# Reordering the first loads of a two-layer transformer kernel: Wq in four pieces, Wv ahead of the transposing DMAs, softmax of group 0 one unit earlier

## The chip, the cores and the metric

The kernel runs on one core of one Trainium2 chip. The metric is the device time of one execution in microseconds (us); lower is better. "Before" is the kernel without the change, "after" the kernel with it.

Engine names are those of the profile: PE is TensorE (matmuls), PEld its weight loads, DVE is VectorE, ACT is ScalarE, POOL is GpSimd, SP is SyncE, which here only issues DMAs (SPq in the traces).

## The reference, cut to what matters

```python
def _A_ref(x, wqkv, wo):                 # attention, 32 heads of 32, window of 8 keys, dilation 2
    qkv = (x @ wqkv) ...
    logits = einsum(q, gathered k) * scale, masked for positions before 0
    o = softmax(logits) @ gathered v
    return o.reshape(B, S, D) @ wo

def _B_ref(x, w1, b1, w2, b2):           # feed-forward, F = 3584
    return gelu(x @ w1 + b1) @ w2 + b2

x = A_x                                  # 1 x 2048 x 1024, bf16
x = x + _A_ref(_layernorm(x), A_wqkv, A_wo)
x = x + _B_ref(_layernorm(x), B_w1, B_b1, B_w2, B_b2)
# ... and the same two lines once more, with the same weights
```

## The kernel before: the parts that matter

The 2048 rows are handled as four groups of 512 rows, that is of four tiles x0 to x3, x4 to x7 and so on, 128 rows each. A group needs Q, K and V (8 chunks of 128 columns each), then the windowed attention on DVE, then Wo. PE is kept in program order; for the other engines a scheduler picks an order when the kernel is built, except where program order is demanded: POOL is in program order from the start on (`pool.on = True`).

```python
x = [xpool.tile([P, D], BF16, name=f"x{t}") for t in range(S // P)]

def load_x(g):                                   # four tiles of 256 KB, on SP
    for tt in range(NTT):
        t = g * NTT + tt
        sp.dma_start(x[t][:], x_in[t * P:(t + 1) * P, :])

load_x(0)

def load_qkv(which):                             # 0 is Wq, 1 is Wk, 2 is Wv; two halves of 1 MB, on SP
    tiles = []
    for h in range(2):
        wt = wpool.tile([P, KD // 2, D], BF16, name="wt")          # 5 buffers
        sp.dma_start(wt[:], wqkv_v[:, h * (KD // 2):(h + 1) * (KD // 2), which * D:(which + 1) * D])
        tiles.append(wt)
    return tiles

wq_first = load_qkv(0)
# ... cut ...

def build_constants():
    pool.memset(zhalo[:], 0.0)                   # zeros for the halo of the first group
    # ... cut: other small constants on POOL ...

def load_bias():
    b1_rows = attp.tile([KF, P], BF16, name="abc")
    pool.dma_start(b1_rows[:], B_b1.rearrange("(j p) -> j p", p=P))        # issued by POOL
    pool.dma_start(b2bc[:], B_b2.unsqueeze(0).to_broadcast([P, D]))
    ps = psum.tile([P, KF], BF16, name="acc", bufs=6)
    pe(nc.tensor.transpose(ps[:], b1_rows[:], ident[:KF, :KF]))            # PE waits for b1 here
    act.copy(b1T[:], ps[:])
```

A layer norm of one tile goes DVE (statistics), POOL (two tiny instructions that make `rstd`), DVE (the norm `xn`, three buffers), and then, for every group but the first, a transposing DMA on SP that reads `xn` and writes `xnT`. So DVE may write the norm of a tile only when the transposing DMA of three tiles back has landed.

```python
def ln_stats(t, mv=None, rstd=None, between=None):
    # ... DVE: bn_stats twice, bn_aggr ...
    pool.tensor_tensor(out=rstd[:], in0=mv[:, 1:2], in1=eps_t[:], op=ALU.add)
    pool.tensor_tensor(out=rstd[:], in0=rstd[:], in1=mhalf[:], op=ALU.pow)
    return mv, rstd

def ln_norm(t, mv, rstd):
    xn = lnp.tile([P, D], BF16, name="xn", bufs=3)
    vec.tensor_scalar(out=xn[:], in0=x[t][:], scalar1=mv[:, 0:1], scalar2=rstd[:], op0=ALU.subtract, op1=ALU.mult)
    return xn

def ln_tile(t, tt, xnT, on_pe=False, ahead=False):
    # ... cut ...
    sp.dma_start_transpose(xnT[:, tt, :, :], xn[:].rearrange("s (k p) -> s k p", p=P))
```

The first group is transposed on PE instead, and its first Q chunks are computed from the first two tiles while the other two are still on their way:

```python
def gen_qkv(n, parts=1, defer=False, qk_pool=None, v_late=False):
    # ... cut ...
    wq = wq_first if n == 0 else load_qkv(0)
    wk = load_qkv(1)
    qT = qk_pool.tile([P, NCH, T], BF16, name="qT")
    first = {}
    for kh in range(2 if n == 0 else 0):               # two half passes over the first two tiles
        for c in range(6):
            first[c] = qkv_chunk(wq, c, xnT, first.get(c), kh * (KD // 2), (kh + 1) * (KD // 2), 0, 2)
            if kh == 1 and c in (0, 3):
                transpose_on_pe(*first_late.pop(0))    # the third and the fourth tile
    for c in range(NCH):                               # "the next pass": the other two tiles
        ps = qkv_chunk(wq, c, xnT, first[c], t0=2) if c in first else qkv_chunk(wq, c, xnT)
        act.copy(qT[:, c, :], ps[:])
        yield
    if not v_late:
        wv = load_qkv(2)
    kT = qk_pool.tile([P, NCH, HALO + T], BF16, name="kT")
    s["qT"], s["kT"] = qT, kT
    act.copy(kT[:, :, 0:HALO], (zhalo if g == 0 else khalo)[:])
    # ... cut: K (8 units), V (8 units), one yield per chunk ...
```

DVE multiplies Q with the shifted K (`new_prod`, 2.2 us each) and adds the products in pairs; `head_sum` is a group of PE matmuls that sums a product over each head. The first head sum stands behind the fourth V chunk in PE's program order, so PE stops there if DVE is not ready. A `stage` runs one generator unit by unit and hangs side work on units:

```python
pool.on = True
warm_up(16)
ln_first()
build_constants()
with tc.tile_pool(name="early", bufs=1) as early:
    load_x(1)
    stage(gen_qkv(0, 2), sides=at(0, load_x, 2) + at(0, ln_a, 1) + at(1, load_x, 3) + at(6, ln_a, 2, early)
          + at(14, load_bias) + at(19, head_sum, 0, False))
    q1 = gen_qkv(1, 2, defer=True, qk_pool=early)
    stage(q1, sides=at(6, attend, 0) + at(6, spread, 0) + at(6, hold) + each(new_prod, 1, 8, 1, 0, 4) + each(av, 0, 12, 1))
    # ... cut ...
```

`attend(0)` makes the softmax of group 0.

## Time and profile before

| what | value |
|---|---|
| time before, median of 3 runs | 1247.69 us (1247.63 to 1249.89) |
| span of the profiled execution | 1246.4 us |
| PE busy | 1236.3 us (99%) |
| PE waiting for the Wqkv loads | 5.4 us, three times |
| first projection matmul | 10.36 us |
| next pass begins | 17.04 us |
| first head sum on PE | 53.62 us |

Two lines of the page: PE's busy time from its first part, and the shares of the chain of waits that ended last.

```profile
PE 1236.3 (99%) x5871; PEld 633.3 (51%) x5871; DVE 836.2 (67%) x864; ACT 305.9 (25%) x477; POOL 95.2 (8%) x215
...
PE 98%; DMA 1%; SPq 0%; ACT 0%; issue 0%; DVE 0%
```

PE is what bounds the kernel, and there is little left but what keeps PE from working at full rate. PE's waits say what that is (engine, the tile waited with, line; what it waited for; us in total, times, longest).

```profile
PE acc L118 <- DMA wt<-in_A_wqkv_dram: 5.4, 3, 2.5
PE acc L118 <- DVE big L93: 1.1, 1, 1.1
PE acc L118 <- ACT xnT L93: 0.2, 1, 0.2
```

The 1.1 us for DVE's big tile are the warm-up's first operand. The 5.4 us are found in PE's timeline (start, us, engine, line, operation, shapes, count, and in brackets the idle time just before and what ended it).

```profile
10.36 3.37 PE L118 MATMUL acc<-xnT,wt 128*128 128x256 bf16 x28 [1.45 <-DMA wt<-in_A_wqkv_dram]
...
17.04 20.94 PE L118 MATMUL acc<-xnT,wt 128*128 128x256 bf16 x120 [0.22 <-ACT xnT L93]
...
41.44 1.09 PE L118 MATMUL acc<-xnT,wt 128*128 128x512 bf16 x4 [1.46 <-DMA wt<-in_A_wqkv_dram]
45.03 8.66 PE L118 MATMUL acc<-xnT,wt 128*128 128x512 bf16 x28 [2.51 <-DMA wt<-in_A_wqkv_dram]
53.62 0.61 PE L118 MATMUL L<-big,smat 128*32 128x512 bf16 x8
```

The waits are 1.45 us at Wq, 1.46 and 2.51 us at the two halves of Wv. Then 28 matmuls take 8.66 us, which is 0.31 us each. The table by stretches says why (stretch, its length, busy us and instructions of PE, PEld, DVE, ACT, POOL, the granted TensorE clock, DMA share, GB/s).

```profile
40.00:50.00 10.00, 6.05 (x16) 2.52 (x17) 9.83 (x6) 1.74 (x4) 0.00 (x0) 0.66 0.95 340
```

The granted clock was 0.66 there. In shorter stretches it was 1.00 for the four matmuls between the two waits (41.44 to 42.53 us), 0.62 during the second wait, 0.50 from 45.03 to 49.70 us, where weight loads start 0.43 us apart, and 0.96 from 49.70 to 53.60. So in this trace two waits of 4.0 us in all are followed by 4.7 us of matmuls at half the clock.

Why the halves of Wv are late is in SP's timeline: they are issued at 33.31 and 36.99 us, behind transposing DMAs (DMA_TRANSPOSE), for `load_qkv(2)` comes after all of Q in the program.

```profile
17.22 7.80 SPq L93 DMA_TRANSPOSE xnT<-xn  x3
...
33.31 0.85 SPq L93 DMA_DIRECT2D wt<-in_A_wqkv_dram  x1
34.25 2.65 SPq L93 DMA_TRANSPOSE xnT<-xn  x1
36.99 4.67 SPq L93 DMA_DIRECT2D wt<-in_A_wqkv_dram  x4
```

DVE's timeline: the norms of x7 and x8, at 25.48 us, wait for nothing; DVE waits once, 1.80 us at the norm of x10, for a transposing DMA to free a norm buffer, and the last two additions for the first head sum end at 47.64 us, 6 us before PE gets there.

```profile
25.48 0.99 DVE L93 TENSOR_SCALAR xn<-x,mv,rstd 128x1024 bf16<-128x1024 bf16 x2
...
30.70 0.63 DVE L93 TENSOR_SCALAR xn<-x,mv,rstd 128x1024 bf16<-128x1024 bf16 x1 [1.80 <-DMA xnT<-xn]
...
43.02 4.62 DVE L93 TENSOR_TENSOR big<-big 128x4096 bf16<-128x4096 bf16 x2
```

### The profile page before, as it was taken

Reading aid. Unit: us, or ns where it says so; the run is one execution under the profiler, and the core shown is the slowest. Engines: PE = TensorE matmul, PEld = TensorE weight load, DVE = VectorE, ACT = ScalarE, POOL = GpSimd, SP = SyncE. Lnnn points to the kernel's source line nnn. Section 1 sums busy time; section 2 is a strip of 40 time slices with the busy share of each in tenths; the row PEclk is TensorE's granted clock in tenths of the full one; section 3 lists DMA queues with packets and bytes.
Section 4 is the critical chain, followed back from the end, with each engine's and each line's share of the span. In section 5 each row is a group of like instructions: output and inputs, shape, how many; then the busy total and the mean of one; then the engine's idle time right before and its main releaser. Section 6 shows DMA issues by size and latency. Waiting matters only on the chain.

```text
span 1246.4 us, 14107 instructions
## 1 busy us (share of the span) xinstructions
PE 1236.3 (99%) x5871; PEld 633.3 (51%) x5871; DVE 836.2 (67%) x864; ACT 305.9 (25%) x477; POOL 95.2 (8%) x215
## 2 busy tenths in 40 slices
PE   9899999999999999999999999999999999999998
PEld 6566544446444564445644456444554444444444
DVE  7969889996995889528994379943598688012001
ACT  3233253013430135201352013510235101310310
POOL 4010112002001100101001010000000002000000
PEclk9899999999999999999999999999999999999999
DMA  9755554586746547656566555666654567546441
GB/s 301 215 191 188 142 190 155 166 206 189 199 147 202 169 137 208 184 165 159 169 185 199 165 164 173 161 198 193 199 155 146 181 202 193 166 155 195 147 138 53
DMA packets 215296, 219.83 MB, mean 176 GB/s; under 512 B 66034, under 2 KB 184960, under 8 KB 212160
## 3 DMA queue, kind: packets, MB, share of 16 engines
q1 hardware_dynamic: 212560, 208.16, 55.7%
q0 software_dynamic: 2672, 10.76, 2.8%
q8 instruction: 46, 0.75, 0.2%
q14 instruction: 18, 0.15, 0.0%
HBM read 197.40 MB, written 6.29 MB: 163 GB/s over the span
## 4 chain that ended last, share of the span: by engine, by line
PE 98%; DMA 1%; SPq 0%; ACT 0%; issue 0%; DVE 0%
PE acc L118 98%; DMA wt<-in_A_wqkv_dram 1%; PE L L118 0%; SPq L93 0%; ACT xnT L93 0%; PE L L206 0%; PE acc L206 0%; DVE x L93 0%
## 5 line engine op out<-in xcount | busy, mean ns | idle before, releaser
L118 PE MATMUL acc<-xnT,wt 128*128 128x512 bf16 (+1 forms) x3376 | 725.6, 377 | 5.6 <-DMA wt<-in_A_wqkv_dram 5.4
L118 PEld LDWEIGHTS <-wt 128*128 128x128 bf16 x3376 | 398.3, 119 | 329.0 <-issue 6.9
L118 PE MATMUL acc<-wt,hT 128*128 128x512 bf16 (+1 forms) x1820 | 388.1, 376 | 0.0
L118 PEld LDWEIGHTS <-hT 128*128 128x128 bf16 x1820 | 178.2, 98 | 208.9
L93 DVE TENSOR_TENSOR big<-big 128x2048 bf16<-128x2048 bf16 (+2 forms) x182 | 239.6, 1349 | 1.6
L93 ACT ACTIVATE hT<-acc,b1T 128x512 bf16<-128x512 f32 x224 | 151.6, 687 | 318.5 <-PE acc L118 318.0
L93 DVE TENSOR_TENSOR big<-abc,vT 128x4096 bf16<-128x4096 bf16 x64 | 143.9, 2283 | 48.5 <-DMA abc<-a_d 48.5
L93 DVE TENSOR_TENSOR big<-qT,kT 128x4096 bf16<-128x4096 bf16 x64 | 144.1, 2286 | 26.4 <-ACT kT L93 23.3
L93 DVE TENSOR_TENSOR tmp<-acc,b2bc 128x512 f32<-128x512 f32 x56 | 38.7, 691 | 178.4 <-PE acc L118 174.7
L93 ACT CAST qT<-acc 128x512 bf16<-128x512 f32 x64 | 37.2, 585 | 328.4 <-PE acc L118 328.4
L118 PE MATMUL acc<-wt,oT 128*128 128x512 bf16 x448 | 97.9, 379 | 0.0
L93 DVE BATCH_NORM_STATS2 stats<-x 128x6 f32<-128x512 bf16 x128 | 84.1, 677 | 4.4 <-DMA x<-in_A_x_dram 3.5
L118 PEld LDWEIGHTS <-oT 128*128 128x128 bf16 x448 | 43.8, 98 | 53.0 <-issue 0.2
L93 DVE TENSOR_TENSOR x<-acc,big 128x512 bf16<-128x512 f32 (+1 forms) x9 | 5.7, 632 | 90.0 <-PE acc L118 90.0
L93 ACT CAST vT<-acc 128x512 bf16<-128x512 f32 x64 | 37.5, 586 | 91.6 <-PE acc L118 91.6
L93 DVE TENSOR_SCALAR xn<-x,mv,rstd 128x1024 bf16<-128x1024 bf16 x60 | 32.7, 546 | 34.1 <-POOL rstd L93 31.3
L93 ACT CAST kT<-acc 128x512 bf16<-128x512 f32 x64 | 37.5, 585 | 72.1 <-PE acc L118 72.1
L93 POOL TENSOR_TENSOR rstd<-mv,eps_t 128x1 f32<-128x1 f32 x60 | 15.1, 251 | 501.4 <-DVE mv L93 501.4
L93 POOL DMA_DIRECT2D a_d<-a x32 | 19.5, 636 | 414.1 <-DVE a L93 414.1
L93 DVE TENSOR_TENSOR x<-acc,x 128x512 bf16<-128x512 f32 x64 | 43.0, 671 | 6.2 <-PE acc L118 5.9
L93 DVE TENSOR_TENSOR x<-tmp,x 128x512 bf16<-128x512 f32 x56 | 38.7, 691 | 1.7
L93 POOL TENSOR_TENSOR rstd<-rstd,mhalf 128x1 f32<-128x1 f32 x60 | 33.8, 563 | 4.7
(54 smaller groups left out, 213.0 us busy)
## 6 DMA issues: line engine op xcount, KB each, us to landing
wt<-in_B_w_dram SPq DMA_DIRECT2D x56, 1024.0 KB, 6.0
wt<-in_B_w_dram SPq DMA_DIRECT2D x64, 896.0 KB, 4.9
wt<-in_A_wqkv_dram SPq DMA_DIRECT2D x48, 1024.0 KB, 5.7
wt<-in_A_wo_dram SPq DMA_DIRECT2D x16, 1024.0 KB, 5.0
abc<-a_d POOLq DMA_DIRECT2D x32, 256.0 KB, 4.9
x<-in_A_x_dram SPq DMA_DIRECT2D x16, 256.0 KB, 6.8
out_dram<-x SPq DMA_DIRECT2D x31, 128.0 KB, 1.8
a_d<-a POOLq DMA_DIRECT2D x32, 64.0 KB, 3.4
```

Of the source, the lines that this page charges most:

```text
L93: inst = f(*args, **kwargs)
L118: return pe(nc.tensor.matmul(*args, **kwargs))
```

## The change

The intent: take PE's 5.4 us of waiting for weights away, and the low clock that follows. Wq's halves come in two pieces each, placed between the first x tiles, and the first pass goes by quarters to match. Wv of group 0 is issued together with Wk and the third group of x, ahead of the transposing DMAs. As PE would then run ahead, the softmax of group 0 is placed at unit 5 of the next group instead of 6.

```diff
-    def load_x(g):
-        for tt in range(NTT):
+    def load_x(g, t0=0, t1=NTT):
+        for tt in range(t0, t1):
...
-    load_x(0)
+    def load_qkv_half(which, h, pieces=1):
+        wt = wpool.tile([P, KD // 2, D], BF16, name="wt")
+        n = KD // 2 // pieces
+        for i in range(pieces):
+            k = h * (KD // 2) + i * n
+            sp.dma_start(wt[:, i * n:(i + 1) * n, :], wqkv_v[:, k:k + n, which * D:(which + 1) * D])
+        return wt
...
-    wq_first = load_qkv(0)
+    load_x(0, 0, 2)
+    wq_first = [load_qkv_half(0, 0, 2)]
+    load_x(0, 2, 4)
+    wq_first.append(load_qkv_half(0, 1, 2))
...
         norm(0)
-        stats[2] = ln_stats(2, between=lambda: norm(1))
+        norm(1)
+        stats[2] = ln_stats(2)
...
         wk = load_qkv(1)
+        if n == 0:
+            load_x(2)
+            wv = load_qkv(2)
...
-        for kh in range(2 if n == 0 else 0):
+        for kq in range(4 if n == 0 else 0):
             for c in range(6):
-                first[c] = qkv_chunk(wq, c, xnT, first.get(c), kh * (KD // 2), (kh + 1) * (KD // 2), 0, 2)
-                if kh == 1 and c in (0, 3):
+                first[c] = qkv_chunk(wq, c, xnT, first.get(c), kq * (KD // 4), (kq + 1) * (KD // 4), 0, 2)
+                if (kq, c) in ((2, 3), (3, 1)):
                     transpose_on_pe(*first_late.pop(0))
...
-        if not v_late:
+        if n > 0 and not v_late:
             wv = load_qkv(2)
...
-        stage(gen_qkv(0, 2), sides=at(0, load_x, 2) + at(0, ln_a, 1) + at(1, load_x, 3) + at(6, ln_a, 2, early)
+        stage(gen_qkv(0, 2), sides=at(0, ln_a, 1) + at(1, load_x, 3) + at(6, ln_a, 2, early)
...
-        stage(q1, sides=at(6, attend, 0) + at(6, spread, 0) + at(6, hold) + ...
+        stage(q1, sides=at(5, attend, 0) + at(5, spread, 0) + at(5, hold) + ...
```

More of the change, by code (lines that the diff above doesn't have):

```diff
@@ L120 @@
     x = [xpool.tile([P, D], BF16, name=f"x{t}") for t in range(S // P)]
-    def load_x(g):
-        for tt in range(NTT):
+    def load_x(g, t0=0, t1=NTT):
+        for tt in range(t0, t1):
             t = g * NTT + tt
             sp.dma_start(x[t][:], x_in[t * P:(t + 1) * P, :])
-    load_x(0)
-    def load_qkv(which):
-        tiles = []
-        for h in range(2):
-            wt = wpool.tile([P, KD // 2, D], BF16, name="wt")
-            sp.dma_start(wt[:], wqkv_v[:, h * (KD // 2):(h + 1) * (KD // 2), which * D:(which + 1) * D])
-            tiles.append(wt)
-        return tiles
-    wq_first = load_qkv(0)
+    def load_qkv_half(which, h, pieces=1):
[5 more added lines that the diff above has]
+        return wt
+    def load_qkv(which):
+        return [load_qkv_half(which, h) for h in range(2)]
+    load_x(0, 0, 2)
+    wq_first = [load_qkv_half(0, 0, 2)]
+    load_x(0, 2, 4)
+    wq_first.append(load_qkv_half(0, 1, 2))
     warm = bigp.tile([P, P], BF16, name="big")
@@ L501 @@
         load_x(1)
-        stage(gen_qkv(0, 2), sides=at(0, load_x, 2) + at(0, ln_a, 1) + at(1, load_x, 3) + at(6, ln_a, 2, early)
+        stage(gen_qkv(0, 2), sides=at(0, ln_a, 1) + at(1, load_x, 3) + at(6, ln_a, 2, early)
               + at(14, load_bias) + at(19, head_sum, 0, False))
         q1 = gen_qkv(1, 2, defer=True, qk_pool=early)
-        stage(q1, sides=at(6, attend, 0) + at(6, spread, 0) + at(6, hold) + each(new_prod, 1, 8, 1, 0, 4) + each(av, 0, 12, 1))
+        stage(q1, sides=at(5, attend, 0) + at(5, spread, 0) + at(5, hold) + each(new_prod, 1, 8, 1, 0, 4) + each(av, 0, 12, 1))
         q2 = gen_qkv(2, defer=True)
```

## The prediction

It was written before the changed kernel had run.

> **What bounds it now.** TensorE. The page's first part has PE busy for 1236.3 of 1246.4 us; the chain of waits is 98% PE. PE's waits list names 5.4 us (three times) for the Wqkv loads.
>
> The timeline splits the 5.4 us. (a) 1.45 us before the first projection matmul at 10.36 us: Wq had not landed; xnT was ready at 10.01. (b) 1.46 us at 39.98 and 2.51 us before 45.03: the halves of Wv of group 0, issued at 33.31 and 36.99 us, behind transposing DMAs. (c) Then the clock is low: the table by stretches grants 0.66 for 40 to 50 us. The 28 matmuls from 45.03 took 8.66 us; at the K phase's 0.216 us each they would take 6.04: 2.6 us lost, and 0.2 us for four between the waits. [...] weight loads 0.43 us apart until 49.7 agree.
>
> **The change** (no arithmetic differs).
>
> 1. Wv early. In the built order its first half precedes the first three transposing DMAs and its second follows them (it waits for the first Wq buffer, free at about 24 us). At 8 us each, both are there by 33 us; needed at 39.5. This removes (b) and (c): 1.46 + 2.51 + 2.6 + 0.2 = 6.8 us, all critical.
>
> 2. Wq in pieces. Its first quarter comes after 0.5 MB of x, so its wait should vanish; matmuls start after half of the second tile's ACT copy, about 9.5 us. Some goes back: only 8 matmuls (0.97 us) part the two late transposes, chained by ACT copies (1.01 us each), so PE waits about 0.4 us. Estimate: 0.5 us won by the next pass (17.04 before).
>
> 3. Given back at the first head sum. It follows the fourth V chunk and moves on PE from 53.6 to about 46.4 us. DVE finished its input at 47.6 us, with only 2 us idle since 25.5. The 1 MB of Wv ahead of the transposes makes these up to 2.7 us later, and DVE's norm tiles wait for them; but the new DVE order puts two products ahead of the fourth such wait. I expect DVE done at 45.6 to 47.5: a PE wait of 0 to 1.2 us, 0.8 in the sum, too short to drop the clock.
>
> 4. Softmax at unit 5. The second head sum comes at about 65 us; DVE's products should end by 63.5 (65.9 before, with 2.3 us of waiting for the first head sum, which goes). No PE wait. DVE needs this lead: its last oT came at 132.0 us, the Wo matmuls at 134.6, and these move 7 us earlier.
>
> Sum: -6.8 - 0.5 + 0.8 = -6.5 us, 0.5%.
>
> **Predicted:** 1241.2 us, 8 in 10 within 1239.6 to 1243.5. Faster by over 2%: 0.5%; within 2%: 99%; slower: 0.5%.
>
> **What would show it.** PE's waits on Wqkv under 0.5 us; clock 1.00 from 40 to 50 us; first projection matmul near 9.5 us; V without a gap; a new PE wait for DVE's "big" tile near 46 us of at most 1.2 us; none at the second head sum or Wo.
>
> **What would make it wrong.** Transposes so delayed that DVE is 2 us late at the first head sum; the clock dropping there; Wk late; a DVE wait passed on to Wo.

The 2.6 us are the measured 8.66 less 28 times 0.216, the time from one matmul of the K phase to the next in before. Of the other figures, "8 us each" is what the halves of Wv took from issue to landing in before (8.1 and 8.0 us), and the 2.7 us of point 3 is what 1 MB comes to at the 388 GB/s moved from 45.03 to 49.70 us in before. That a PE wait of 0 to 1.2 us is "too short to drop the clock" no trace had shown by then; runs made later do: the clock of 40 to 60 us was 1.00 with waits of 0.65 (e5) and of 1.56 and 1.03 us (e2) in it.

## More of the kernel before

`ln_a(1)` norms x4 to x7 and `ln_a(2)` x8 to x11. Both come before `load_bias` in the program, so on POOL the loads of b1 and b2 stand behind the `rstd` pairs of all eight tiles.

POOL's timeline: the last `rstd` pair takes 0.19 and 0.55 us, and the load of b1 ("abc<-in_B_b_dram") is issued right behind it, at 29.75 us. PE transposes b1 at 37.91 us and does not wait for it.

```profile
28.98 0.19 POOL L93 TENSOR_TENSOR rstd<-mv,eps_t 128x1 f32<-128x1 f32 x1 [0.52 <-DVE mv L93]
29.25 0.55 POOL L93 TENSOR_TENSOR rstd<-rstd,mhalf 128x1 f32<-128x1 f32 x1
29.75 0.74 POOL L93 DMA_DIRECT2D abc<-in_B_b_dram  x1
```

## The result, and the profile after

| kernel | median us | lowest to highest, runs | granted clock, mean of the span |
|---|---|---|---|
| before, the same rounds | 1248.79 | 1247.63 to 1251.38, 4 | not listed |
| after | 1247.18 | 1245.43 to 1247.52, 4 | 0.998 (the profiled run, 1247.52 us), 0.998, 1.000, 0.999 |

The ratio is 0.9981, with a 95% interval from 0.9961 to 1.0002: the same time. A ratio here and below is the mean time of one kernel's runs over that of the other's of the same rounds, so it is not quite the ratio of the medians. The time predicted was 1241.2 us, at most 1243.5 with the range; the median is 6.0 us above the prediction and 3.7 us outside its range.

PE's waits after the change:

```profile
PE acc L179 <- DMA abc<-in_B_b_dram: 3.6, 1, 3.6
PE L L210 <- ACT xnT L93: 1.8, 1, 1.8
PE acc L118 <- DVE big L93: 1.1, 1, 1.1
PE acc L118 <- ACT xnT L93: 0.9, 2, 0.7
```

The waits for Wqkv are gone, all of them. Instead PE waits 3.6 us for the 7 KB of b1, which nobody had waited for before, and 1.8 us in the head for an ACT copy. PE's timeline:

```profile
9.42 3.82 PE L118 MATMUL acc<-xnT,wt 128*128 128x256 bf16 x32 [0.67 <-ACT xnT L93]
...
16.44 0.61 PE L210 MATMUL L<-ident,xn 128*128 128x128 bf16 x8 [1.78 <-ACT xnT L93]
...
18.15 20.94 PE L118 MATMUL acc<-xnT,wt 128*128 128x256 bf16 x120 [0.22 <-ACT xnT L93]
42.73 0.18 PE L179 MATMUL acc<-ident,abc 28*128 28x28 bf16 x1 [3.64 <-DMA abc<-in_B_b_dram]
42.85 10.54 PE L118 MATMUL acc<-xnT,wt 128*128 128x512 bf16 x40
53.32 0.61 PE L118 MATMUL L<-big,smat 128*32 128x512 bf16 x8
```

The first projection matmul starts 0.94 us earlier (9.42 against 10.36), but the next pass starts 1.11 us later (18.15 against 17.04). The first head sum starts at 53.32 us, only 0.30 us earlier than before. The table by stretches:

```profile
40.00:50.00 10.00, 7.27 (x27) 3.95 (x28) 7.88 (x5) 1.95 (x6) 0.00 (x0) 0.83 1.01 279
```

The clock is low in that stretch again, 0.83: it was 0.50 from 43.6 to 46.6 us, behind the wait for b1, and 0.99 from 46.6 to 53.3. Now the engines behind PE. DVE's timeline:

```profile
28.60 0.55 DVE L93 TENSOR_SCALAR xn<-x,mv,rstd 128x1024 bf16<-128x1024 bf16 x1 [1.98 <-DMA xnT<-xn]
...
31.65 2.24 DVE L93 TENSOR_TENSOR big<-qT,kT 128x4096 bf16<-128x4096 bf16 x1
...
33.92 2.24 DVE L93 TENSOR_TENSOR big<-qT,kT 128x4096 bf16<-128x4096 bf16 x1
...
42.06 0.55 DVE L93 TENSOR_SCALAR xn<-x,mv,rstd 128x1024 bf16<-128x1024 bf16 x1 [2.70 <-DMA xnT<-xn]
...
47.04 4.62 DVE L93 TENSOR_TENSOR big<-big 128x4096 bf16<-128x4096 bf16 x2
```

The norm of x7, which needs the buffer that x4's transposing DMA reads, starts at 28.60 us after a wait (25.48 before, without one); the norm of x11 waits again, 2.70 us, for x8's. DVE's input of the first head sum is complete at 51.66 us (47.04 + 4.62) instead of 47.64. Why the transposing DMAs are late is in SP's timeline:

```profile
15.50 0.38 SPq L93 DMA_DIRECT2D wt<-in_A_wqkv_dram  x1
18.83 9.87 SPq L93 DMA_TRANSPOSE xnT<-xn  x3
28.80 0.53 SPq L93 DMA_DIRECT2D wt<-in_A_wqkv_dram  x1
```

Wv's first half, 1 MB, stands ahead of the three transposing DMAs, and the issue of these three now takes 9.87 us instead of 7.80. The megabyte, issued at 15.50 us, landed 12.1 us later, at about 27.6 us, and the first transposing DMA after it, at about 28.5 us. That is 9.7 us after its own issue at 18.83, against 7.5 us before.

POOL's timeline shows how this gets to b1:

```profile
31.81 2.12 POOL L93 TENSOR_TENSOR rstd<-mv,eps_t 128x1 f32<-128x1 f32 x1 [1.53 <-DVE mv L93]
34.01 2.56 POOL L93 TENSOR_TENSOR rstd<-rstd,mhalf 128x1 f32<-128x1 f32 x1
...
37.51 0.74 POOL L93 DMA_DIRECT2D abc<-in_B_b_dram  x1
```

The `rstd` pair of x10, the last tile but one, takes 2.12 and 2.56 us instead of 0.19 and 0.55, exactly while DVE runs its two products (31.65 to 33.89, 33.92 to 36.16). The first of the pair ends at 33.93, when the first product does, and the second at 36.57, 0.4 us after the second product. In before the pairs were over (29.80) before DVE's first product began (31.25). So b1's load, behind one more pair on POOL, is issued at 37.51 instead of 29.75 us, 7.8 us later. The long pair is not all of it. DVE finished the statistics of x11, which that last pair needs, 5.1 us later than before (they are gathered at 33.80 us, behind the first product, against 28.70); the other 2.7 us we put down to the long pair, an estimate from these times. The load takes 5.2 us to land in both kernels; PE needed it at 39.1.

The 1.8 us in the head are another matter. ACT's timeline:

```profile
15.01 0.28 ACT L93 COPY kT<-zhalo 128x112 bf16<-128x112 bf16 x1 [5.16 <-POOL zhalo L93]
15.20 0.28 ACT L93 COPY vT<-zhalo 128x112 bf16<-128x112 bf16 x1
15.39 1.00 ACT L93 COPY xnT<-L 128x1024 bf16<-128x1024 bf16 x1
```

The scheduler placed the two halo copies on ACT ahead of the copy of the third tile's transposition, as it had in before. They wait for a memset on POOL that stands behind the `rstd` of x3, and x3 is later now, as two pieces of Wq are loaded ahead of x2 and x3: that memset ran at 12.19 us in before and at 14.79 us in after. So ACT's copy, whose input PE had written by 13.8 us, starts at 15.39, and PE's next transposition waits for it.

### Two accounts that fit so far

From the next pass to the first head sum PE's work is the same in all kernels here with the head sum at its place. Without a wait and at clock 1.00 it takes 29.87 us; this was measured later, in the kernel e9_xn_bufs (18.18 to 48.05 us); e1, e5 and e8, their wait taken off, give 29.84 to 29.85. What is left over after the waits is the loss to the low clock.

| us | before | after | as predicted |
|---|---|---|---|
| next pass begins | 17.04 | 18.15 | 16.54 |
| work to the first head sum | 29.87 | 29.87 | 29.87 |
| waits in it | 1.46 + 2.51 | 3.64 | 0.8 |
| left over: the low clock | 2.74 | 1.66 | 0 |
| first head sum begins | 53.62 | 53.32 | 47.2 |

Two theories for the loss were set against each other. **Theory A:** the late load of b1 is the whole loss; move it, and the predicted gain comes. **Theory B:** DVE is late because of the transposing DMAs, and b1 only shows it first; PE would ask for the first head sum at 18.15 + 29.87 = 48.02 us, and DVE is ready at 51.66, so that a second wait of about 3.6 us stands hidden behind the first.

### The profile page after: what moved, and what is told of

The parts are those of the page before. It is cut to its first block, busy times and chain, and to the rows that moved or that the text cites. A ratio compares the mean times of both kernels' runs of the same rounds, so it can differ in the third digit from the quotient of the medians.

```text
span 1245.8 us, 14060 instructions
## 1 busy us (share of the span) xinstructions
PE 1232.6 (99%) x5821; PEld 633.5 (51%) x5871; DVE 835.9 (67%) x864; ACT 306.2 (25%) x477; POOL 99.1 (8%) x215
## 4 chain that ended last, share of the span: by engine, by line
PE 96%; DMA 2%; DVE 1%; POOL 1%; issue 0%; SPq 0%; DVEq 0%
PE acc L118 96%; DMA xnT<-xn 1%; POOL rstd L93 1%; DMA x<-in_A_x_dram 1%; PE L L118 0%; DMA abc<-in_B_b_dram 0%; DVE stats L93 0%; DVE xn L93 0%; SPq L93 0%; DVE mv L93 0%; PE acc L210 0%; DVE x L93 0%; PE acc L179 0%; DVEq L93 0%
```

## The experiments

Fourteen runs were made, each of five rounds (e7 and e8 of six runs), all correct. Those told together ran on the same chip and share the runs of before. Diffs are against after, if nothing else is said. A plain fourth norm buffer in the pool of the other three did not fit in the memory there and was not run (after does not build with it: a later pool asks for 28 KB per partition and 26.4 are left); e9 takes its two from another pool.

### First set: where does the loss sit?

**e1_b1_early:** the loads of b1 and b2 are issued on POOL right behind the constants, ahead of the `rstd` pairs; PE's transposition stays where it was.

```diff
-    def load_bias():
-        b1_rows = attp.tile([KF, P], BF16, name="abc")
-        pool.dma_start(b1_rows[:], ...); pool.dma_start(b2bc[:], ...)
+    def fetch_bias():                      # the two loads alone
+        ...
+    def load_bias():                       # transposition and copy, at unit 14 as before
...
     build_constants()
+    b1_rows = fetch_bias()
```

> The changed kernel with only the loads of b1 and b2 moved on POOL's queue, from behind the eight rstd pairs to ahead of them; every other engine keeps its order. Theory A (PE's 3.64 us wait for b1, and the half clock after it, are the loss): that wait and the clock drop vanish, the time falls by about 5.5 us (3.6 + 1.9) against the changed kernel. Theory B (the b1 wait hides a second one: DVE ends the input of the first head sum only at 51.66 us, and without the b1 wait PE wants it at about 47.9): PE shows a wait of about 3.8 us for DVE's big tile at 47.9 us, the first head sum stays at about 51.7 to 53 us, and the time falls by 0 to 2 us.

Measured: 1247.99 us (1246.91 to 1248.87) against 1247.56 of before; ratio 1.0000 [0.9987, 1.0013]. The wait for b1 is gone, and this line of PE's timeline is there:

```profile
52.10 0.61 PE L118 MATMUL L<-big,smat 128*32 128x512 bf16 x8 [3.85 <-DVE big L93]
```

DVE was done at 52.05 us and the clock of 50 to 60 us was 0.83. The 3.64 us at b1 came back as 3.85 us at the head sum, with its own clock loss. Theory A falls: taking the visible wait away gained nothing.

**e2_x3_late:** the load of x12 to x15, which stood in SP's order ahead of the transposing DMAs of x8 to x10, goes from unit 1 to unit 20. **e3_b1_x3** is e1 and e2 together.

```diff
-  at(1, load_x, 3)
+  at(20, load_x, 3)
```

> The changed kernel with only the loads of the last four x tiles moved to unit 20, behind the transposing DMAs of group 2's first tiles. Both theories: the POOL chain in front of b1 is untouched, so PE still waits about 3.6 us for b1 and the time is the same within 1 us. Theory B adds: DVE's 2.7 us wait for a transposing DMA at 39.4 us vanishes, and DVE ends the first head sum's input near 49 us instead of 51.7.

> Both edits, b1 early and the last x tiles late. Theory A: the same as b1 early alone (about -5.5 us against the changed kernel, no more). Theory B: only now does the time fall: no b1 wait, a wait for DVE's big tile of about 1.1 us near 47.9 us, no clock drop, about -4.4 us against the changed kernel, and 2 to 5 us better than b1 early alone.

Measured: e2 1245.94 us (1244.67 to 1246.73), ratio 0.9982 [0.9970, 0.9995]; b1's wait fell to 1.56 us, a wait of 1.03 us appeared at the head sum, no clock drop, first head sum at 50.46 us. e3: 1247.31 us (1247.05 to 1248.64), ratio 0.9996 [0.9984, 1.0009]: a miss against the expectation. In e3 the wait at the head sum was 3.98 us, DVE waited for norm buffers three times (2.21, 0.98 and 1.82 us), and x7's norm still came only at 28.76 us. The loads of x12 to x15 are thus a part of the second wait for buffers, but not the cause of the first, and as long as the first is there, moving b1 helps nothing.

**e4_head_old:** the old head (loads of x and Wq, two half passes, the old order of statistics), with the early Wv kept.

```diff
-    load_x(0, 0, 2)
-    wq_first = [load_qkv_half(0, 0, 2)]
-    load_x(0, 2, 4)
-    wq_first.append(load_qkv_half(0, 1, 2))
+    load_x(0)
+    wq_first = load_qkv(0)
# and the two half passes and the statistics of before
```

> The changed kernel with the start as before: Wq in two loads behind all four x tiles, two half passes, statistics interleaved as before. If the start's loss of 1.1 us is the Wq pieces' doing, PE begins the rest of the chunks at 17.0 us again instead of 18.15. Theory B: the time does not follow, for b1 still comes late (its POOL chain waits for DVE and DVE for the transposes): PE's b1 wait grows by about the 1.1 us, time the same within 1 us. If instead the start counts in full, the time falls by 1.1 us.

Measured: 1246.28 us (1246.20 to 1247.99), ratio 0.9989 [0.9975, 1.0002]. The next pass began at 16.99 us, 1.16 us earlier than in after, but the time did not follow: b1's load was issued at 38.99 us, PE waited 3.86 us for it, and the clock of 40 to 50 us was 0.66. A better start earns nothing as long as PE then waits for something that does not follow PE's own pace.

### Second set: Wv behind the first transposing DMAs

**e5_wv_mid:** Wv of group 0 is loaded after the second Q chunk, which puts it behind the first three transposing DMAs on SP.

```diff
         if n == 0:
             load_x(2)
-            wv = load_qkv(2)
...
             act.copy(qT[:, c, :], ps[:])
+            if n == 0 and c == 1:
+                wv = load_qkv(2)
             yield
```

> The changed kernel with only the place of group 0's Wv load moved: behind chunk 1 of Q instead of ahead of everything, so that the first three transposing DMAs go ahead of its first half (still some 8 us earlier than in the kernel before). Theory B (the 1 MB of Wv in front of the transposes delays them, and through DVE's norm tiles both b1 and the first head sum): DVE's wait for the first transposing DMA ends near 25.5 us instead of 28.6; POOL issues the b1 load near 31 us instead of 37.5 and PE shows no b1 wait over 0.5 us; DVE ends the first head sum's input at 46 to 48 us, PE's wait for it is at most 1 us; no clock drop; time about -5 us against the changed kernel, about 1242. Rival (the transposes are late for another reason, such as the start or the x tiles): DVE still starts at 28 us or later, waits of over 3 us stay, and the time is within 1.5 us of the changed kernel.

Measured: 1243.47 us (1243.05 to 1244.07) against 1248.83 of before; ratio 0.9957 [0.9945, 0.9969]. The norms of x7 and x8 came at 26.08 us, without a wait (x7 at 28.60 in after):

```profile
26.08 0.99 DVE L93 TENSOR_SCALAR xn<-x,mv,rstd 128x1024 bf16<-128x1024 bf16 x2
```

b1's load was issued at 32.51 us, nobody waited for b1 or Wv, PE waited 0.65 us at the first head sum (48.84 us), and the clock was 1.00 throughout; every one of its five runs had a mean clock of 1.00. With the megabyte behind the transposes the time falls by 0.24 points of the ratio against after (0.9981, on another chip), some 3 us. This supports Theory B, but moves SP's order of everything; e9 below is the sharper test.

**e6_wv_mid_u6** is e5 with the softmax of group 0 at unit 6, as in before.

```diff
-  at(5, attend, 0) + at(5, spread, 0) + at(5, hold)
+  at(6, attend, 0) + at(6, spread, 0) + at(6, hold)
```

> The same with the softmax of group 0 back at unit 6. Expected: the same time within 0.7 us, the second head sum 1.7 us later on PE, no PE wait at Wo, since DVE had 2.6 us in hand there in the kernel before and gains as much as PE does. If unit 5 mattered, PE would wait for DVE's oT at Wo.

Measured: 1243.28 us (1242.79 to 1244.13), ratio 0.9955 [0.9943, 0.9967]. The second head sum came at 69.07 us instead of 66.81, and PE waited for nothing at it, nor at Wo. Softmax at unit 5 is worth nothing measurable, and costs nothing.

**e7_mid_old** is e5 with e1, e2 and the old head. **e8_mid_zhalo** is e5 with e1, e2, the new head, and the memset of the halo's zeros put at the head of POOL's order:

```diff
     def build_constants():
-        pool.memset(zhalo[:], 0.0)
...
+    pool.memset(zhalo[:], 0.0)             # when the constants' tiles are made
     b1T = const.tile([P, KF], F32, name="b1T")
```

> Wv behind chunk 1, b1 early, last x tiles late, and the old start. With no PE wait downstream to swallow it, the old start should now count: rest of the chunks from 17.0 us, PE's wait at the first head sum under 1 us, time about 1 us below the Wv-behind-chunk-1 kernel, about 1240.7.

> The same with the new start, but zeroing of the halo tile moved to the head of POOL's queue. Theory: in the changed kernel the ACT copy of the third x tile (15.39 us) stood behind ACT's two halo copies, which waited for POOL's memset at 14.79, which stood behind the fourth tile's rstd; so PE's 1.8 us wait before the fourth tile's transposes was ACT's. Expected: that copy at about 13.8 us; the wait falls to about 0.8 us (the fourth tile's norm ends at 15.4), rest of the chunks from about 17.2 us instead of 18.15, time within 0.7 us of the old start. Rival (Wq pieces ahead of x tiles 2 and 3 alone cost it): still 18.0 us or later.

Measured: e7 1246.45 us (1244.18 to 1248.16, six runs), ratio 0.9979 [0.9967, 0.9990], a miss. Its next pass began early, at 16.63 us, but DVE waited 2.36 us for the tile x8 and 1.78 and 1.93 us for norm buffers, was done at 51.14 us, PE waited 4.72 us at the head sum and the clock of 50 to 60 us was 0.67. The issue of its first three transposing DMAs took 10.05 us although Wv stood behind them (6.52 us in e5); why is open. e8: 1242.88 us (1242.55 to 1244.89, six runs), ratio 0.9957 [0.9945, 0.9969]. With the zeros made first, ACT's copy of the third tile started at 14.00 us instead of 15.39, the transposition behind it waited 0.28 us instead of 1.78, and the next pass began at 16.85 us (18.35 in e5): this is what had turned the head's gain into a loss. Still e8 is only 0.6 us below e5, for PE, 1.5 us earlier, waited 1.90 us at the head sum instead of 0.65: DVE was done at 48.54 us in e8 and 48.79 in e5. DVE, not PE, now sets when the first head sum starts.

### Third set: the norm buffers themselves, and the head alone

**e9_xn_bufs** leaves the loads of after as they are, Wv ahead of the transposes. It only gives the norms of x7 and x8 two further buffers, from a pool that is there anyway. So DVE need not wait for a transposing DMA there.

```diff
-        xn = lnp.tile([P, D], BF16, name="xn", bufs=3)
+        xn = extra[0].tile([P, D], BF16, name="xne", bufs=2) if extra and t in (7, 8) else lnp.tile([P, D], BF16, name="xn", bufs=3)
...
         load_x(1)
+        extra.append(early)
```

> The changed kernel with two more buffers for DVE's normalised tiles (x tiles 7 and 8); the DMA queue keeps Wv's first half ahead of the transposing DMAs, as in the changed kernel, up to the eighth transpose. Theory B says that Wv in front of the transposes costs only through the buffers: DVE may not write a norm tile before a transposing DMA three tiles back has landed. With five buffers DVE waits only for the first three transposes (landing near 28.5 to 30.5 us), then runs its four products and three sums without a wait: first head sum's input done at 46.5 to 48 us instead of 51.7; b1 load issued near 30 us instead of 37.5; PE's b1 wait 0, wait at the first head sum under 1 us, no clock drop; about 5 us below the changed kernel, 1242 to 1243. Rival (Wv's bytes slow something else, such as Wk or the x tiles): PE waits over 3 us stay.

Measured: 1241.73 us (1241.14 to 1242.40) against 1248.96 of before; ratio 0.9943 [0.9930, 0.9955]. No wait for b1, none at the first head sum, clock 1.00 in all five runs. PE's timeline:

```profile
18.18 20.94 PE L118 MATMUL acc<-xnT,wt 128*128 128x256 bf16 x120 [0.22 <-ACT xnT L93]
39.06 0.18 PE L179 MATMUL acc<-ident,abc 28*128 28x28 bf16 x1
39.17 8.86 PE L118 MATMUL acc<-xnT,wt 128*128 128x512 bf16 x40
48.05 0.61 PE L118 MATMUL L<-big,smat 128*32 128x512 bf16 x8
```

DVE was done at 47.99 us (43.37 + 4.62), and POOL's last `rstd` pair was short again and b1's load followed it:

```profile
43.37 4.62 DVE L93 TENSOR_TENSOR big<-big 128x4096 bf16<-128x4096 bf16 x2
...
30.54 0.39 POOL L93 TENSOR_TENSOR rstd<-mv,eps_t 128x1 f32<-128x1 f32 x1 [0.29 <-DVE mv L93]
31.01 0.55 POOL L93 TENSOR_TENSOR rstd<-rstd,mhalf 128x1 f32<-128x1 f32 x1
31.51 0.74 POOL L93 DMA_DIRECT2D abc<-in_B_b_dram  x1
```

The first three transposing DMAs are about as slow as in after (9.19 us of issue, 9.87 in after), with Wv ahead of them, but nobody waits for them:

```profile
18.87 9.19 SPq L93 DMA_TRANSPOSE xnT<-xn  x3
```

Both waits, the one for b1 and the hidden one, are gone with one edit that touches neither. This shows Theory B: the loss came from the shortage of norm buffers. One thing is not separated. With the two buffers the scheduler also chose another order for DVE: all norms up to x11 come before the first product, while in after the norm of x10 stands behind two products. So the edit removes DVE's waits and changes its order at once. e14 below, with the same buffers and a third order (the norm of x11 behind two products), has no buffer wait either and comes out alike.

**e11_head_only** is before with the new head alone (the loads of Wq in pieces, the quarter passes, the order of the statistics), nothing of Wv.

> The kernel before with the change's start alone (Wq in four pieces, the second tile's norm first). Expected: rest of the chunks from about 18 us instead of 17.04 (ACT's copy behind the halo copies); the time does not follow, since Wv's landing at 45 us and not PE's arrival ends the wait: the Wv waits shrink by the same 1 us, time within 1 us of the kernel before. If the start counts in full, the time rises by 1 us.

Measured: 1250.57 us (1249.45 to 1250.76), ratio 1.0010 [0.9998, 1.0023]. The next pass began at 18.21 us, as in after: the 1.1 us later start belongs to the new head alone. The waits for Wv were 3.63 and 1.96 us (1.46 and 2.51 in before). The median is 1.6 us higher, but the interval holds 1.

**e12_after_again** is after once more, on this chip; the edit is none.

> The changed kernel once more, in the same rounds as the others, so that their differences from it can be read on one chip: 1246 to 1248 us, about 0.2% below the kernel before; runs near 1245.5 when the clock happens not to drop after the b1 wait.

Measured: 1247.41 us (1246.83 to 1249.47), ratio 0.9987 [0.9973, 1.0001]. Here b1's load, issued at 37.84 us, landed at 44.11, PE waited 5.40 us, and the clock was 0.66. So the size of this wait varies from run to run, its place and the result do not.

**e10_best** puts together e9's buffers, e5's Wv and e8's zeros, but not e1's early b1.

> What the theory points to: the changed kernel with Wv behind chunk 1 of Q, the two more buffers, and the halo tile zeroed first. Expected: rest of the chunks from 16.9 us, DVE done with the first head sum's input at 44 to 46 us, PE waits under 0.5 us at b1 and at the first head sum, second head sum without a wait; time 1241 us (1.9 us below the halo run's 1242.9), the fastest of all.

Measured: 1245.69 us (1244.15 to 1247.92), ratio 0.9973 [0.9960, 0.9985]: a miss, 4 us slower than e9. PE's waits in it:

```profile
PE acc L179 <- DMA abc<-in_B_b_dram: 3.6, 1, 3.6
```

b1's load was issued at 33.83 us, 2.3 us later than in e9, and took 8.1 us to land (6.0 in e9, 5.2 in after). The DMA engines moved 389 to 404 GB/s from 30 to 36 us there (253 to 298 in e9): both halves of Wv and x12 to x15 were under way. DVE was done with the head sum's input at 50.32 us. This profile fell on the slowest of the five runs (1247.92 us, mean clock 0.997); two of them ran at clock 1.00 and took 1244.15 and 1244.17 us.

### Fourth set: what made e10 miss, and the best version

**e13_best_b1** is e10 with b1 early (the edit of e1): it tells whether b1's late landing alone was the loss.

> e10_best with the bias loads issued ahead of the rstd pairs on POOL; nothing else differs. If the late bias load alone was the loss of e10_best: no TensorE wait for the bias, none over 0.5 us at the first head sum, VectorE done with its input before 48.5 us, clock 1.0, time 1240.5 to 1242. If VectorE is late as well, which I expect (its input was done at 50.32 us in e10_best, and TensorE without the bias wait wants it near 47): a new wait of about 3 us at the first head sum, VectorE done near 50 us, time 1244 to 1245.5.

Measured: 1244.94 us (1243.71 to 1247.31) against 1249.60 of before; ratio 0.9964 [0.9951, 0.9977]. PE's timeline:

```profile
49.47 0.61 PE L118 MATMUL L<-big,smat 128*32 128x512 bf16 x8 [2.87 <-DVE big L93]
```

As in e1, the wait moved from b1 to the head sum. It was 2.87 us, DVE was done at 49.42 us, and the time is nearly e10's. So b1's 8.1 us were not the loss. DVE was late: it waited 3.4 us for POOL's `rstd` between 20 us and the head sum (2.0 us in e9). The likely reason, read from the traces and not tested, is that the order that the scheduler chose there has less work between a tile's statistics and its norm. With Wv behind the transposes the two buffers brought no gain here: DVE was ready at 48.54 us in e8, without them.

**e14_final** is e9, with the zeros first (e8), b1 early (e1) and the first head sum one V chunk later.

```diff
# on top of e9_xn_bufs, with the edits of e1 and the memset of e8
-  at(19, head_sum, 0, False)
+  at(20, head_sum, 0, False)
```

> The change with two more norm buffers (e9_xn_bufs), and the memset of the halo's zeros ahead on POOL, the bias loads ahead, and the first head sum one chunk later. If the loss at the start counts and nothing else gives way: halo copies no longer hold up ACT's copy of xnT, next pass from 16.9 to 17.5 us (18.18 in e9_xn_bufs), no wait for the bias, under 0.5 us at the first head sum, clock 1.0, time about 1240.5, some 1.2 us below e9_xn_bufs' 1241.73. If the earlier start is eaten by VectorE again: next pass as early, but a wait of 1 us or more at the head sum, and the time as e9_xn_bufs, 1241.2 to 1242.5.

Measured: 1241.25 us (1240.62 to 1241.77), ratio 0.9932 [0.9918, 0.9945], against 0.9943 [0.9930, 0.9955] of e9 on another chip. The next pass began at 17.49 us (18.18 in e9), no wait for b1, none at the head sum, clock 1.00 in all five runs; the span of the profiled execution was 1239.8 us against 1240.7. The profiled spans differ by about the 0.7 us won at the start, and the medians by 0.5, but the intervals of the two ratios overlap: that e14 is faster than e9 is likely and not shown. It is the fastest version, 0.7% below before.

### All runs on one page

| kernel | median us | ratio to before | next pass | PE's wait at b1, at the first head sum | DVE ready for it |
|---|---|---|---|---|---|
| before | 1248.79 | 1 | 17.04 | 0, 0 (Wv: 1.46 + 2.51) | 47.64 |
| after | 1247.18 | 0.9981 | 18.15 | 3.64, 0 | 51.66 |
| e1_b1_early | 1247.99 | 1.0000 | 18.40 | 0, 3.85 | 52.05 |
| e2_x3_late | 1245.94 | 0.9982 | 17.96 | 1.56, 1.03 | 50.41 |
| e3_b1_x3 | 1247.31 | 0.9996 | 17.71 | 0, 3.98 | 51.48 |
| e4_head_old | 1246.28 | 0.9989 | 16.99 | 3.86, 0 | 50.60 |
| e5_wv_mid | 1243.47 | 0.9957 | 18.35 | 0, 0.65 | 48.79 |
| e6_wv_mid_u6 | 1243.28 | 0.9955 | 17.99 | 0, 1.54 | 49.33 |
| e7_mid_old | 1246.45 | 0.9979 | 16.63 | 0, 4.72 | 51.14 |
| e8_mid_zhalo | 1242.88 | 0.9957 | 16.85 | 0, 1.90 | 48.54 |
| e9_xn_bufs | 1241.73 | 0.9943 | 18.18 | 0, 0 | 47.99 |
| e10_best | 1245.69 | 0.9973 | 17.51 | 3.56, 0 | 50.32 |
| e11_head_only | 1250.57 | 1.0010 | 18.21 | 0, 0 (Wv: 3.63 + 1.96) | 47.80 |
| e12_after_again | 1247.41 | 0.9987 | 17.77 | 5.40, 0 | 52.31 |
| e13_best_b1 | 1244.94 | 0.9964 | 16.76 | 0, 2.87 | 49.42 |
| e14_final | 1241.25 | 0.9932 | 17.49 | 0, 0 (one chunk later) | 48.46 |

The last column sorts the ratios well. Among the kernels with the change's early Wv, those with DVE ready at 49.33 us or before have ratios of 0.9957 or less, those at 49.42 us or after have 0.9964 or more. But each DVE time is that of one profiled run, and at the border, e6 and e13, the intervals of the ratios overlap.

## Why the prediction was wrong, point by point

**What bounds it, and points (b) and (c): right.** PE bounds the kernel, and the two waits for Wv and the low clock after them were worth what was said. e9 shows it: from the next pass to the head sum it needs 29.87 us against 36.58 in before, a gain of 6.71 us where (b) and (c) gave 6.8. Of (a), the wait before the first projection matmul, see step 2.

**1. Wv early: the waits went, the gain did not stay.** The waits for Wqkv vanished from PE's list, as predicted, and the removed time was on the critical path, as e9 shows. But "V without a gap" and "clock 1.00 from 40 to 50 us" were wrong: a wait of 3.64 us for b1 opened at the head of V, and the clock was 0.83.

**2. Wq in pieces: wrong in sign.** The first projection matmul came at 9.42 us, as predicted (9.5). The next pass was to begin 0.5 us earlier than before, at 16.54 us, and began 1.11 us later, at 18.15. The prediction allowed PE a wait of 0.4 us between the two late transpositions; it was 1.78 us. It had looked at ACT's copies alone and not at what stood ahead of them on ACT: two halo copies that wait for POOL's memset behind the `rstd` of x3, a tile that the change itself makes later. e11 shows that the head alone does this, e8 that the memset is the cause (0.28 us of wait with it moved). With the memset moved, the head still wins next to nothing over before: the next pass began at 16.76 to 17.51 us in e8, e10, e13 and e14, against 17.04.

**3. Given back at the first head sum: this is the step that failed, by its size and in what it left out.** It said that the transposes would be "up to 2.7 us later", that DVE would be done "at 45.6 to 47.5: a PE wait of 0 to 1.2 us, 0.8 in the sum, too short to drop the clock". The mechanism was right: Wv ahead, transposes later, norms waiting for their buffers. The first delay was of about the size named, 3.1 us at x7's norm (28.60 against 25.48; 2.5 us in e4, which has the old head). The rest was not:
- The lateness did not shrink on its way. x7's own transposing DMA, and those of x8 to x10 behind four loads of x, were later too. The prediction counted on two products ahead of the fourth norm that needs such a buffer, and they did cover it: the norm of x10 waited only 0.44 us, for `rstd`. It left out the fifth, the norm of x11, with one sum ahead of it: that waited another 2.70 us for a buffer, up to 42.06 us. DVE was done at 51.66 us, 4.2 us after the latest time said.
- It had a second way out that the prediction did not follow. The late norms put POOL's `rstd` pairs under DVE's products, where they took 2.12 and 2.56 us instead of 0.19 and 0.55, and b1's load, behind them on POOL, was issued 7.8 us later than before (5.1 us from DVE's lateness, 2.7 by our estimate from the long pair). PE asks for b1 before it asks for the head sum. So the loss showed as a wait for b1, with DVE's own wait of about 3.6 us hidden behind it; e1 made it visible (3.85 us).
- After that wait of 3.64 us the clock was low again, 0.50 from 43.6 to 46.6 us: 1.66 us more.

In the sum of the prediction this term was 0.8 us; it measured 3.64 + 1.66 = 5.3 us, 4.5 us more. With the 1.6 us of step 2 (18.15 against 16.54) this makes 6.1 us at the first head sum (53.32 against 47.2), and the time was 6.0 us above the prediction. The condition named under "What would make it wrong", DVE 2 us late at the first head sum with the clock dropping, is what happened. It had been given too little weight: the range ended 2.3 us above the prediction.

**4. Softmax at unit 5: right that no wait comes, wrong that DVE needs the lead.** e5 and e6 agree within 0.2 us, and no kernel here waits at Wo. In e6, without the lead, DVE's last oT was done at 127.85 us and Wo began at 130.36: 2.5 us in hand, as in before (132.10 and 134.61).

**What stays open.** Why e10 and e13, with less in front of the transposes, leave DVE later than e9: the longer waits for `rstd` (3.8 and 3.4 us against 2.0) cover most of e10's 2.3 us and e13's 1.4, and that they come from the scheduler's order was read from the traces, not tested by pinning that order. Nor was e9's order of DVE pinned, with or without the buffers. Why b1's 7 KB took 8.1 us in e10 and 5.2 in after: the queue was fuller, but no run changed that alone. And that DVE's products hold up POOL's `rstd` pairs is read from their times alone (2.12 and 2.56 us under two products in after, 0.19 and 0.55 ahead of them in before); no run took the products away while leaving the rest.

## What to carry to other kernels

A load issued ahead of transposing DMAs is not free because its bytes fit in time (here the issue of three of them took 9.87 us instead of 7.80): ask what buffers these transposes free, who needs them, and follow that engine's lateness to every wait of the bounding engine, in that engine's order, not to the nearest one alone. When a new wait appears where an old one was taken away, compare the time at which the *next* thing would have been ready before moving it; here the cheap-looking repair (the bias load) gained nothing (ratio 1.0000 against before, 0.9981 for after), and with two more buffers the kernel came to 0.9943, about the predicted time. An earlier start of the bounding engine counted for little where a wait behind it was ended by another engine (e4, e8).

## What was measured of the hardware on the way

- Plain bytes queued ahead of DMA transposes. The issue of the first three transposing DMAs took 9.19 to 10.78 us in six kernels with 1 MB of Wv ahead of them (9.87 in after, and there the first landed 9.7 us after its issue), and 6.52 to 7.80 us in six with Wv behind (7.80 in before, where the first landed after 7.5; 6.52 in e5); a seventh with Wv behind, e7, took 10.05. Each is one profiled run.
- A small load on POOL's queue beside SP's traffic. b1's 7 KB took 5.2 us to land in before and after, 6.0 in e9, and 8.1 us in e10, where the engines moved 389 to 404 GB/s as it was issued.
- Small POOL instructions under DVE's products. An `rstd` pair of 0.19 and 0.55 us took 2.12 and 2.56 us in after, with the same numbers to 0.01 us in e1, e2, e3, e4 and e12, which we estimate to be 2.7 of the 7.8 us by which a DMA issue behind it in POOL's order came later in after.
- Waits of PE and the clock behind them. Single waits of 3.56 to 5.40 us (after, e1, e3, e4, e7, e10, e12) came with a clock between 0.66 and 0.83 in the stretch of ten microseconds in which they ended, the one of 2.87 us in e13 did not (1.00). But in before two waits of 1.46 and 2.51 us with 1.1 us of work between them did it as well (0.66). From which length or spacing on this happens was not measured. And it varies between runs of one kernel: after took 1245.43 us at a mean clock of 1.000 and 1247.52 us at 0.998.
